# The order of the first transfers: gates by three queues, first words on two, then values and GpSimd's clearing of memory

## The chip, the cores and the metric

The kernel runs on one core of a Trainium2 chip. The metric is the device time of the whole kernel in microseconds (us), as the median of several executions. One more execution is taken with the hardware profiler; the span of its instructions and the durations of single operations come from that one.

## The reference

Four sequences, eight heads, 768 positions, head size 48. A recurrence with a complex gate for each position and head dimension makes the attention output, and a feed-forward block with a squared ReLU follows. All inputs and the output are float32.

```python
mag = np.sqrt(a_re * a_re + a_im * a_im)
scale = np.minimum(mag, 0.999) / (mag + 1e-06)
a_re_n, a_im_n = a_re * scale, a_im * scale
for t in range(S):                                  # S = 768
    new_re = ar * S_re - ai * S_im                  # ar, ai: the gates at t
    new_im = ar * S_im + ai * S_re
    kv = np.einsum('bhd,bhe->bhde', k[:, :, t], v[:, :, t])
    S_re, S_im = (new_re + kv, new_im)
    y[:, :, t] = np.einsum('bhd,bhde->bhe', q[:, :, t], S_re)

x = y.transpose(0, 2, 1, 3).reshape(3072, 384)
h = np.maximum(x @ w_in, 0.0)                       # w_in 384 x 2048
out = h * h @ w_out                                 # w_out 2048 x 384
```

The two weight matrices reach the chip as 64-bit floats, that is as pairs of 32-bit words, and are turned into 32-bit floats on VectorE.

## The kernel before, in words

**Tiling.** A chunk is 128 positions of one sequence; a group is one chunk of each of two sequences. There are 24 chunks in 12 groups. The heads lie in pairs on the partitions: 64 rows for each of two heads, of which 48 hold head dimensions and the 16 left over (the `pads`) hold a third each of the fourth pair of heads. The tile `raw` holds the gates (real and imaginary), the queries and the keys of a group; `vt` holds the values, two tiles for each of two groups.

**A list of tokens.** The order of the work on every engine is written out by hand as one list of tokens, `FRONT`. `follow` calls one small function for each token, and each engine's queue gets its instructions in the order in which these functions issue them. The tokens that matter here, with a group's or block's number behind the letter:

- `l0.0` loads the gates of the first group (`load_parts` with part 0); `l0.1` and `i0.1` load its queries and keys, the first head's half on SP, the other on GpSimd (POOL). `l1`, `i1` load the next group whole.
- `v0`, `v1` load values (`load_values`), two transfers each on SP.
- `f0` to `f15` fetch a block of weight words: for w_in the upper partitions' half on SP with `f`, and the lower half on POOL with `j`. There are three buffers for blocks.
- `W0`... let ScalarE watch the size of a block's words (L600, L602); `D0`... decode a block on VectorE in five operations (L587, L589, L591, L594 and a sum, L480).
- `M0` loads ScalarE's table and `M1` turns the mask.
- `o0.k` is step k of a group's operands. `o0.0` squares the gates on ScalarE (L700), `o0.3` sums them on VectorE (L713), `o0.4` (L718) and `o0.5` (L722) are the first inverse and its square on ScalarE, `o0.7` is the inverse on VectorE (L480, L731). `o0.8`, `o0.9`, `o0.10` are the limit, the lessened factor and the grown factor on ScalarE (two L685 and L745), `o0.11` makes the gates (L751 to L755), `o0.22` is L764 to L767, `o0.13` the scan (L771), `o0.14` the keys (L776, L685).
- `a0.k` and `b0.k` are the steps of a group's two chunks: 0 the scores (L872), 1 to 4 the keys turned and copied to `kt` (L879, L883, L884), 5 the masking (L480), 6 the sums of values (L898), 7 the tokens (L907), 8 the products to be added (`add`, L919), 9 the new state.
- `F`, `H` and the capital letters behind them are the feed-forward block.

VectorE's list begins with some small fills, then `o0.3`, `o0.7`, `D0`, `o0.11`, `D1`, `o0.13` and so on. ScalarE begins with its share of the gates' transfers, then `M0`, `o0.0`.

**The first transfers.** The gates of one chunk and one head are a large transfer of 144 KB (48 rows) and two of 24 KB (the pads). SP issues those of the first head of each pair and ScalarE those of the other: twelve in all, six on each. SP goes on with the four value transfers (192 KB each), its half of `f0` (192, 96 and 96 KB), then its half of the queries and keys. Transfers from SP and ScalarE share eight semaphores, and those from POOL have eight others, so that each issue waits until the transfer that used its semaphore eight issues before has landed.

**What POOL does first.** It clears the last 16 columns of the four `vt` tiles (L487), makes the identity and the mask, and clears `qk`, `last`, `prod`, the states, `kt` and `begun` (L558 to L571). Then come its halves of `f0` and of the queries and keys.

The profile's lines are those of the kernel before; in the changed kernel most stand one line earlier.

Of the kernel before, what the change touches and what calls it, by code (L numbers as in the profile page):

```python
# [44 lines left out]
def gap_rows(hh, d):  # L45
    return slice(hh * ROWS + d, (hh + 1) * ROWS)
# [379 lines left out]
def quotient_path(ctx, tc, feat, vtok, w_in, w_out, w1, w2, out, n_seq, count):  # L426

    nc = tc.nc
    N, _, D, _, NP, C = feat.shape
    DM, FF = w_in.shape  # L430
# [11 lines left out]
    W = C + 2  # L442
# [18 lines left out]
    def rows(hh):  # L461
        return head_rows(hh, D)
# [7 lines left out]
    def pads(hh):  # L470
        return gap_rows(hh, D)
# [11 lines left out]
    raw = const.tile([P, 4, GC, NG, C], F32, name="raw")  # L483

    vt = [const.tile([C, DM + PAD], F32, name=f"vt{i}") for i in range(2 * GC)]
    for t in vt:
        nc.gpsimd.memset(t[:, DM:], 0.0)  # L487


    TWO_QUEUES = 3  # L490
# [1 line left out]
    def load_parts(gi, part=None, second=False):  # L492


        parts = [slice(A_RE, Q), slice(Q, V), slice(A_RE, V)][2 if part is None else part]
        queues = [nc.sync, nc.scalar if part == 0 else other if gi < TWO_QUEUES else nc.sync]
        if part != 0 and gi < TWO_QUEUES:
            queues[not second] = None
        for b, n in enumerate(groups[gi]):
            for hh, queue in enumerate(queues):  # L500
                if queue is None:
                    continue
                queue.dma_start(
                    out=raw[rows(hh), parts, b].rearrange("d x g t -> d x (g t)"),
                    in_=feat[n, hh, :, parts, 0:NG].rearrange("d x g t -> d x (g t)"))

                gap = raw[pads(hh), parts, b]
                rest = feat[n, hh].rearrange("(r g) x p t -> r x g p t", g=NG)[:, parts, :, NG]
                for i in range(min(gap.shape[1:3])):
                    at = (slice(None), i) if gap.shape[1] < NG else (slice(None), slice(None), i)  # L510
                    queue.dma_start(out=gap[at], in_=rest[at])
# [23 lines left out]
    def turn_mask(step):  # L535
        if step == 0:

            nc.scalar.activation(out=sums[:, 0:1], in_=tiny, func=AF.Abs_reciprocal_sqrt)
            return
        nc.scalar.copy(out=mask.rearrange("p (j n) -> p n j", j=L),  # L540
                       in_=plain.rearrange("p (n j) -> p n j", j=L))
        turned = pm.tile([C, C], F32, tag="m", name="turned")
        nc.tensor.transpose(turned, mask, ident)
        nc.scalar.copy(out=mask.rearrange("p (j n) -> p n j", j=L),
                       in_=turned.rearrange("p (n j) -> p n j", j=L))
# [8 lines left out]
    qk_of = [const.tile([P, 4, GC, NG, W], F32, name=f"qk{i}") for i in range(2)]  # L554
    last = [const.tile([P, 4, GC, W], F32, name=f"last{i}") for i in range(2)]
    prod = [const.tile([P, 3, GC, NP], F32, name=f"prod{i}") for i in range(2)]
    for t in qk_of:
        nc.gpsimd.memset(t[:, :, :, :, C:W], 0.0)  # L558

    states = [[const.tile([P, 2, NP, ROWS], F32, name=f"state{b}{i}") for i in range(2)]  # L560
              for b in range(GC)]
    for t in last + prod + states[0] + states[1]:
        nc.gpsimd.memset(t, 0.0)
    kt = [const.tile([C, NP, P], F32, name=f"kt{i}") for i in range(2)]
    for t in kt:
        nc.gpsimd.memset(t, 0.0)

    sums = const.tile([P, NGR], F32, name="sums")
    ends = const.tile([P, NGR, SEG], F32, name="ends")
    begun = const.tile([P, E], F32, name="begun")  # L570
    nc.gpsimd.memset(begun, 0.0)  # L571
    sizes = const.tile([P, 2, 2 * NBLK], F32, name="sizes")
    nc.vector.memset(sizes, 1.0)
    tiny = const.tile([P, 1], F32, name="tiny")
# [467 lines left out]
    def outputs(i, r):  # L1042
# [27 lines left out]


    FRONT = (
        "l0.0 M0 j0 v0 v1 f0 o0.0 l0.1 i0.1 o0.3 o0.1 o0.4 o0.5 o0.7 o0.2 M1 o0.8 D0 f1 j1 o0.9 "
        "o0.10 o0.6 o0.11 f2 j2 W0 W1 D1 o0.22 f3 j3 o0.12 W2 o0.13 o0.15 o0.14 f4 j4 W3 l1 i1 "
        "o0.16 W4 o0.17 D2 o0.18 o1.6 o0.19 f5 j5 o0.20 o1.0 W5 a0.1 o1.3 o0.21 o1.1 D3 a0.2 "
        "a0.3 o1.4 a0.4 a0.8 o1.5 o1.2 o1.7 f6 j6 b0.0 a0.9 o1.8 b0.1 b0.5 o1.9 b0.6 D4 b0.2 "
        "b0.3 b0.7 a0.0 b0.4 o1.10 W6 b0.8 o1.11 f7 j7 a0.5 o1.12 o1.22 a0.6 b0.9 o1.13 W7 v2 "
        "a0.7 o1.15 o1.14 g0 l2 i2 o1.16 F0.0 o1.17 F0.1 H0.0 D5 o1.18 F0.2 H0.1 o2.6 o1.19 f8 "
        "F0.3 H0.2 F0.4 H0.3 o1.20 o2.0 F0.5 H0.4 W8 a1.1 o2.3 o1.21 D6 a1.2 a1.3 o2.1 a1.4 "
        "a1.8 o2.4 o2.2 F0.6 D7 f9 H0.5 o2.5 a1.0 H0.6 a1.9 F0.7 a1.5 W9 f10 o2.7 a1.6 b1.1 "  # L1080
        "a1.7 D8 b1.0 o2.10 o2.8 H0.7 b1.5 o2.9 f11 b1.6 D9 b1.2 b1.3 b1.7 T0.0 b1.4 g1 W10 "
        "o2.11 T0.1 W11 f12 F1.0 D10 o2.12 o2.22 F1.1 H1.0 D11 T0.2 H1.1 f13 W12 F1.2 o2.15 "
# [61 lines left out]
    def ranges(step):  # L1144
# [35 lines left out]
        "f": fetch,  # L1180
        "j": lambda i: fetch(i, True),
        "i": lambda gi, part=None: load_parts(gi, part, True),
        "D": weights,
        "W": lambda i: watch(words_of[i], i) if i in words_of else None,
        "t": sum_weights,
        "l": load_parts,
        "v": load_values,
        "M": turn_mask,
        "K": ranges,
    }  # L1190
# [13 lines left out]
@with_exitstack  # L1204
def kernel(
    ctx: ExitStack,
    tc: tile.TileContext,
    feat: bass.AP,
    vtok: bass.AP,
    w_in: bass.AP,  # L1210
    w_out: bass.AP,
    out: bass.AP,
    n_seq: int,
):
    nc = tc.nc
    DM, FF = w_in.shape
    wts = ctx.enter_context(tc.tile_pool(name="wts", bufs=1))
    w1 = wts.tile([P, DM // P, FF], F32, name="w1")
    w2 = wts.tile([P, FF // P, DM], F32, name="w2")
    count = wts.tile([1, 1], I32, name="count")  # L1220
    quotient_path(tc, feat, vtok, w_in, w_out, w1, w2, out, n_seq, count)
    n_good = nc.values_load(count, min_val=0, max_val=P)
    with tc.If(n_good < P):
        decode_weights(tc, w_in, w_out, w1, w2, feat.shape[2])
        general_path(tc, feat, vtok, w1, w2, out, n_seq)
# [30 lines left out]
```

## Time and profile before

| | |
|---|---|
| median of 4 runs | 707.35 us (707.0 to 708.59) |
| profiled execution, its own time | 706.3 us |
| its span, first to last instruction | 704.6 us |
| mean granted TensorE clock | 0.986 |
| TensorE busy | 618.9 us (88%) |
| VectorE busy | 524.4 us (74%) |
| ScalarE busy | 386.3 us (55%) |
| GpSimd busy | 36.1 us (5%) |
| moved by DMA | 47.75 MB, mean 68 GB/s |

Times inside the program are counted from the start of the span. Shares are means over stages that differ: the first 100 us, in which the weights are decoded and the first group's operands are made, look unlike the rest. A timeline line has the start, the duration (of the whole run of equal instructions, "x4"), the engine, the source line, the operation with what it writes and reads, and in brackets the engine's idle time before it and what ended that. SPq, POOLq or ACTq mark the issue of a transfer on a queue; the transfer itself lands later. The trace also holds a record for each landing.

### The profile page before, as it was taken

Reading aid. Unit: us, or ns where it says so; the run is one execution under the profiler, and the core shown is the slowest. Engines: PE = TensorE matmul, PEld = TensorE weight load, DVE = VectorE, ACT = ScalarE, POOL = GpSimd, SP = SyncE. Lnnn points to the kernel's source line nnn. Section 1 sums busy time; section 2 is a strip of 40 time slices with the busy share of each in tenths; the row PEclk is TensorE's granted clock in tenths of the full one; section 3 lists DMA queues with packets and bytes.
Section 4 is the critical chain, followed back from the end, with each engine's and each line's share of the span. In section 5 each row is a group of like instructions: output and inputs, shape, how many; then the busy total and the mean of one; then the engine's idle time right before and its main releaser. Section 6 shows DMA issues by size and latency. Waiting matters only on the chain.

```text
span 704.6 us, 12510 instructions
## 1 busy us (share of the span) xinstructions
PE 618.9 (88%) x4955; PEld 544.1 (77%) x4955; DVE 524.4 (74%) x916; ACT 386.3 (55%) x684; POOL 36.1 (5%) x91
## 2 busy tenths in 40 slices
PE   0006489999889999999999999999999999999995
PEld 0005377776578898998999989989989989989895
DVE  1999999999699786896785885995986976872130
ACT  6638387744648537537457557366476475340330
POOL 6331200000000000000000000000000000000000
PEclk9999699999999999999999999999999999999999
DMA  6973634471334062061161051141240330110101
GB/s 168 189 135 77 142 74 142 148 111 39 68 76 64 5 97 68 2 134 30 29 113 23 29 113 25 53 93 20 75 80 11 86 71 9 29 23 2 29 1 28
DMA packets 44164, 47.75 MB, mean 68 GB/s; under 512 B 6016, under 2 KB 39104, under 8 KB 44096
## 3 DMA queue, kind: packets, MB, share of 16 engines
q1 hardware_dynamic: 41408, 41.35, 27.8%
q0 software_dynamic: 2208, 5.11, 3.7%
q8 instruction: 41, 0.67, 0.4%
q10 hardware_dynamic: 480, 0.39, 0.2%
q14 instruction: 27, 0.22, 0.1%
HBM read 36.18 MB, written 4.72 MB: 58 GB/s over the span
## 4 chain that ended last, share of the span: by engine, by line
PE 74%; DVE 14%; DMA 4%; ACT 4%; SPq 2%; issue 1%; DVEq 0%; ACTq 0%
PE h_ps L961 30%; PE o_ps L1038 26%; PE a_ps L872 6%; PE y L898 3%; PE y L864 3%; PE add L919 3%; DMA raw<-in_feat_dram 2%; DVE ab L480 2%; DVE pr L480 2%; PE tp L879 2%; DVE room L480 1%; PE o_ps L977 1%; DVE qk L480 1%; DMA words<-in_moe_w_in_dram 1%; DVE decoded L589 1%
## 5 line engine op out<-in xcount | busy, mean ns | idle before, releaser
L961 PE MATMUL h_ps<-x,w 128*128 128x256 f32 x1152 | 257.1, 383 | 6.8 <-DMA x<-x 6.8
L961 PEld LDWEIGHTS h_ps<-x,w 128*128 128x128 f32 x1152 | 220.0, 192 | 37.9 <-issue 6.0
L966 ACT ACTIVATE h<-h_ps 128x512 f32<-128x512 f32 x96 | 57.5, 599 | 103.5 <-PE h_ps L961 95.4
L1038 PE MATMUL o_ps<-w,h 128*128 128x192 f32 x640 | 111.1, 328 | 0.0
L1038 PEld LDWEIGHTS o_ps<-w,h 128*128 128x128 f32 x640 | 103.6, 190 | 1.8 <-issue 0.9
L480 DVE TENSOR_TENSOR pr<-ab 128x384 f32<-128x384 f32 (+2 forms) x168 | 66.4, 413 | 4.4 <-ACT ab L759 0.5
L967 ACT ACTIVATE h<-h 128x512 f32<-128x512 f32 x96 | 60.6, 631 | 3.0
L879 PE MATMUL tp<-ident,qk 128*128 128x128 f32 x120 | 22.0, 294 | 43.9 <-DVE qk L480 42.0
L480 DVE TENSOR_TENSOR a<-a_ps,mask 128x1024 f32<-128x1024 f32 x24 | 29.4, 1224 | 38.6 <-PE a_ps L872 38.4
L480 DVE TENSOR_TENSOR mix<-h 128x256 f32<-128x256 f32 x40 | 16.9, 423 | 53.6 <-ACT h L967 53.6
L1038 PE MATMUL o_ps<-w_sum,mix 128*128 128x192 f32 x320 | 55.8, 328 | 0.0
L1038 PEld LDWEIGHTS o_ps<-w_sum,mix 128*128 128x128 f32 x320 | 52.0, 190 | 1.1 <-DVE state L480 0.7
L879 PEld LDWEIGHTS tp<-ident,qk 128*128 128x128 f32 x120 | 13.6, 144 | 49.9 <-issue 42.9
L480 DVE TENSOR_TENSOR ab<-pr 128x192 f32<-128x192 f32 (+1 forms) x180 | 45.8, 277 | 4.6
L480 DVE TENSOR_TENSOR qk<-ab,qk 128x768 f32<-128x768 f32 x48 | 44.9, 957 | 0.9
L685 ACT ACTIVATE qk<-raw 128x768 f32<-128x768 f32 x24 | 36.7, 1530 | 15.1 <-DVE raw L480 8.9
L977 PE MATMUL o_ps<-w,h 128*128 128x384 f32 x128 | 42.4, 488 | 0.0
L872 PE MATMUL a_ps<-qk 48*128 48x128 f32 x576 | 39.6, 285 | 0.0
L685 ACT ACTIVATE ab<-raw 128x768 f32<-128x768 f32 x24 | 37.1, 1565 | 2.4 <-DVE qk L480 2.4
L872 PEld LDWEIGHTS a_ps<-qk 48*128 48x128 f32 x576 | 35.0, 192 | 4.2 <-issue 4.2
L480 DVE TENSOR_TENSOR room<-ab,carry 128x1344 f32<-128x1344 f32 x24 | 36.3, 1552 | 2.2 <-ACT carry L800 2.2
L977 PEld LDWEIGHTS o_ps<-w,h 128*128 128x128 f32 x128 | 24.1, 190 | 16.2 <-DVE w L480 0.7
(106 smaller groups left out, 805.7 us busy)
## 6 DMA issues: line engine op xcount, KB each, us to landing
raw<-in_feat_dram SPq DMA_DIRECT2D x40, 288.0 KB
words<-in_moe_w_out_dram SPq DMA_DIRECT2D x8, 768.0 KB
last<-qk SPq DMA_DIRECT2D x72, 64.5 KB
vt<-in_vtok_dram SPq DMA_DIRECT2D x24, 192.0 KB
out_dram<-o SPq DMA_DIRECT2D x24, 192.0 KB
raw<-in_feat_dram SPq DMA_DIRECT2D x120, 32.0 KB
words<-in_moe_w_in_dram POOLq DMA_DIRECT2D x8, 192.0 KB, 4.9
words<-in_moe_w_in_dram SPq DMA_DIRECT2D x8, 192.0 KB
```

The lines of the kernel that those rows point to most:

```text
L480: nc.vector.tensor_tensor(out=out, in0=in0, in1=in1, op=op)
L685: nc.scalar.activation(out=out.rearrange("p c j n -> p c n j"), func=AF.Copy, in_=in_.rearrange("p c (n j) -> p c n j", j=L), **kwargs)
L864: nc.tensor.matmul(ys[p_ % 2][crossed(hh, p_), p_ // 2], lhsT=states[b][1 - c_seq % 2][rows(hh), c, p_], rhs=operand(c, p_, rows(hh)), sta ...
L872: nc.tensor.matmul(ps[:, hh, p_], lhsT=operand(2 + c, p_, rows(hh)), rhs=operand(c, p_, rows(hh)), start=(c == RE), stop=(c == IM))
L879: nc.tensor.transpose(tp[:, g], operands[gi][:, 2 + c, b, g, 0:C], ident)
L898: nc.tensor.matmul(tiles["y"][p_ % 2][crossed(hh, p_), p_ // 2], lhsT=v[:, at:at + ROWS], rhs=tiles["am"][:, hh, p_], start=(first and p_ ...
L919: nc.tensor.matmul(add[rr, c, p_], lhsT=kt[c][:, p_, rr], rhs=v[:, at:at + D], start=True, stop=True)
L961: nc.tensor.matmul(ps[:, j], lhsT=w1[:, g, (2 * f + j) * P:(2 * f + j + 1) * P], rhs=x_of[i][:, g], start=(g == 0), stop=(g == NG - 1))
L966: nc.scalar.activation(out=h, in_=h_ps[i, f], func=AF.Relu)
L967: nc.scalar.activation(out=h, in_=h, func=AF.Square)
L977: nc.tensor.matmul(o_of[i, b], lhsT=tokens_of(i, f, b)[:, j], rhs=w2[:, k], start=(k == 0), stop=(k == NFB - 1))
L1038: nc.tensor.matmul(to, lhsT=x(k)[:, j], rhs=factor(z)[:, 2 * k + j], start=(z in (0, 1, 3) and k == j == 0), stop=(k == KH // 2 - 1 and j ...
```

## The change

Three things are changed, all in what is issued at the start.

1. The small transfers (pads) of the gates of the group's second chunk are issued by POOL and no longer by SP and ScalarE. SP and ScalarE then issue four transfers of the gates each and POOL four.
2. In the list, `f0 j0` follow the gates at once; then come the queries and keys, `f1 j1`, the clearing, `f2 j2`, and only then the values `v0`. `v1` stands behind `f3`.
3. The clearing of memory by POOL, `vt`'s columns included, becomes a step `M2` of the list, in another order (`begun` first), between POOL's halves of `f1` and `f2`. The identity and the mask stay ahead of all.

Apart from this two steps change place further back: `o1.5` comes ahead of `a0.4`, and `b0.2` ahead of `b0.5`. The order of VectorE's instructions stays as it was.

```diff
-    for t in vt:
-        nc.gpsimd.memset(t[:, DM:], 0.0)
...
                     in_=feat[n, hh, :, parts, 0:NG].rearrange("d x g t -> d x (g t)"))
 
+                if part == 0 and b:
+                    queue = nc.gpsimd
                 gap = raw[pads(hh), parts, b]
...
             nc.scalar.activation(out=sums[:, 0:1], in_=tiny, func=AF.Abs_reciprocal_sqrt)
+            return
+        if step == 2:
+
+            for t in ([begun] + [t[:, :, :, :, C:W] for t in qk_of] + last + [t[:, DM:] for t in vt]
+                      + kt + prod + states[0] + states[1]):
+                nc.gpsimd.memset(t, 0.0)
             return
...
-    for t in qk_of:
-        nc.gpsimd.memset(t[:, :, :, :, C:W], 0.0)
...
-    for t in last + prod + states[0] + states[1]:
-        nc.gpsimd.memset(t, 0.0)
...
-    for t in kt:
-        nc.gpsimd.memset(t, 0.0)
...
-    nc.gpsimd.memset(begun, 0.0)
...
-        "l0.0 M0 j0 v0 v1 f0 o0.0 l0.1 i0.1 o0.3 o0.1 o0.4 o0.5 o0.7 o0.2 M1 o0.8 D0 f1 j1 o0.9 "
-        "o0.10 o0.6 o0.11 f2 j2 W0 W1 D1 o0.22 f3 j3 o0.12 W2 o0.13 o0.15 o0.14 f4 j4 W3 l1 i1 "
-        "o0.16 W4 o0.17 D2 o0.18 o1.6 o0.19 f5 j5 o0.20 o1.0 W5 a0.1 o1.3 o0.21 o1.1 D3 a0.2 "
-        "a0.3 o1.4 a0.4 a0.8 o1.5 o1.2 o1.7 f6 j6 b0.0 a0.9 o1.8 b0.1 b0.5 o1.9 b0.6 D4 b0.2 "
...
+        "l0.0 M0 f0 j0 l0.1 i0.1 f1 j1 M2 f2 j2 v0 o0.0 o0.3 o0.1 o0.4 o0.5 o0.7 o0.2 M1 o0.8 "
+        "D0 o0.9 o0.10 o0.6 o0.11 W0 W1 D1 o0.22 f3 v1 j3 o0.12 W2 o0.13 o0.15 o0.14 f4 j4 W3 "
+        "l1 i1 o0.16 W4 o0.17 D2 o0.18 o1.6 o0.19 f5 j5 o0.20 o1.0 W5 a0.1 o1.3 o0.21 o1.1 D3 "
+        "a0.2 a0.3 o1.4 o1.5 a0.4 a0.8 o1.2 o1.7 f6 j6 b0.0 a0.9 o1.8 b0.1 b0.2 b0.5 o1.9 b0.6 "
...
```

## The prediction

> **What bounds the kernel now.** I read the page's tenths first, then the waits of VectorE (DVE), then the timeline of the first 30 us, and last the chain of waits up to 204 us.
>
> The page's tenths, one digit per 17.6 us:
>
> ```profile
> PE   0006489999889999999999999999999999999995
> DVE  1999999999699786896785885995986976872130
> DMA  6973634471334062061161051141240330110101
> ```
>
> TensorE is full only from the seventh slice on. In the first six VectorE shows 9s from the second slice: it sets the pace there, and everything that TensorE does later hangs on it. The first slice, 0 to 17.6 us, has a 1 for VectorE and a 6 for DMA. What VectorE waits for up to 70 us:
>
> ```profile
> DVE room L713 <- ACT room L700: 7.8, 1, 7.8
> DVE decoded L587 <- DMA words<-in_moe_w_in_dram: 4.5, 1, 4.5
> DVE room L480 <- ACT room L722: 2.1, 1, 2.1
> ```
>
> Three waits, all before 19 us: for the gates and ScalarE's squares, for the inverse, and 4.5 us for the first block of words. The timeline says where they come from:
>
> ```profile
> 1.97 1.89 POOL L563 MEMSET last<- 128x1040 f32 x2
> ...
> 3.89 1.95 POOL L563 MEMSET state<- 128x512 f32 x4
> ...
> 5.18 2.70 SPq L520 DMA_DIRECT2D vt<-in_vtok_dram  x4
> ...
> 7.37 1.80 POOL L633 DMA_DIRECT2D words<-in_moe_w_in_dram  x3
> ...
> 7.82 1.48 ACT L700 ACTIVATE room<-raw 128x1536 f32<-128x1536 f32 x1 [0.84 <-DMA vt<-in_vtok_dram]
> 7.93 1.58 SPq L633 DMA_DIRECT2D words<-in_moe_w_in_dram  x3
> ...
> 13.37 0.96 DVE L731 SCALAR_TENSOR_TENSOR z<-room,z 128x768 f32<-128x768 f32 x1
> ...
> 18.82 0.56 DVE L587 TENSOR_SCALAR decoded<-words 128x768 int32<-128x768 int32 x1 [4.49 <-DMA words<-in_moe_w_in_dram]
> ```
>
> The words are issued only at 7.4 (POOL, behind its memsets) and 7.9 us (SP, behind the four vt transfers), and the landing records put their last piece at 18.7 us. The gates land at 7.67, when ACT L700 can begin. From 18.82 to 62 us VectorE has no wait over 0.1 us, and the chain goes through it: each microsecond won ahead of 18.82 is handed on. From 104 us the chain is mostly TensorE's, with pieces of VectorE, ScalarE and DMA up to 204 us, each released by its predecessor and none by a clock.
>
> **The Trainium skill.** "DMA: Bandwidth & Descriptors", section on queues, rings and completion order, says that each DMA engine takes turns between the queues that have work. The trace agrees: from 8 to 15 us POOL's queue moved 24 to 107 KB in each us beside SP's 112 to 178. The same page's section on the GpSimd path puts the fixed cost of a transfer at some 2.0 us. Here the first POOL transfer (7.37) has its first packet at 8.91 and a first landing at 10.22, 2.9 us. "SBUF — State Buffer", section "Who interferes with whom", says that a VectorE operation in a two-port mode (tensor_scalar can be) and GpSimd lock each other out for a whole instruction. No stretch of the trace before has a memset beside such an operation, so I bound that below.
>
> **The change part by part.**
>
> *Gates by three queues.* Each chunk's gates are a large and two small transfers per head. SP and ACT used to issue all twelve; four waited for the landing of earlier ones (eight transfers can be out on their two queues), the last being issued at 4.84 and landing at 7.67. Now the four small ones of the second chunk go by POOL, and ACT and SP issue four each without a wait. The last large one, issued at 2.89, landed at 6.35. POOL reaches its four after the identity and the mask, about 1.8 us (vt's memsets, 0.25, are gone from in front): 4 x 0.52 (row L511 POOL) or 0.24 more with the first issue's price of 0.76, so to 3.9-4.1. With 2.9 us from an issue to its first landing, the last, issued near 3.4, lands about 6.7 to 7.2. ACT is ready before: its two small issues (1.21 us) are gone, so the table load (1.28) ends near 4.6. I take 6.9 us for the gates against 7.82: **-0.9**. Bounds: -1.5 (the large one alone decides, 6.35), +0.9 (POOL's land at 8.7, since some of its other transfers took 4.5 to 8 us in traffic).
>
> *First words on two queues, before the values.* SP's words now stand right after its four gates and wait only for the landing of the first three transfers (3.8 to 4.9), so about 4 to 5.6 us instead of 7.93; POOL's at 4 to 5.7 instead of 7.37. The block is 768 KB; the windows show 222 GB/s from 8 to 16 us: 3.5 us of data, with the second half of the features interleaved, so by 10.5 (11.5 at the worst). VectorE comes to the decode when the inverse is done: before, 6.51 us after L700 began (7.82 to 14.33), so now at 13.4. The words are there: **-4.5**, the whole wait. What is late next is the gates themselves. The sum so far is 5.4: the decode starts at 13.4 for 18.8.
>
> *Is the cover still there behind it?* Decode one (4.1 us) ends at 17.6; ScalarE's limit, lessened and grown factor, which came at 17.56 and 18.20, come at 16.6 and 17.3. Decode two starts at about 21.1 and needs block f1, which landed at 25.47. In front of it on POOL's queue lie 96 KB of gates, 384 of f0 and 384 of features; with f1's own 384 these last three took from 8.9 (first packet) to 23.1 before, 14.2 us. From 5.4 on they give 19.6, 1.5 us in time; SP's half is earlier, since 768 KB of values are out of its way. No cost taken; if POOL's queue starves, up to 2 us.
>
> *The clearing of memory.* Seventeen memsets, some 5.9 us (0.80 to 1.05 and 1.83 to 7.45), move on POOL from ahead of f0 to behind f1's issues, thus about 12.5 to 18.4. Behind them is f2's POOL half, issued at 18.68 before, now 18.4 to 20. It lands near 23; ScalarE watches it (W2) at 25, decode three wants it at 38. Who reads what is cleared comes later: begun at about 24 (cleared first), qk and prod at 38, kt and last at 50 or more. Nothing waits. But the first decode now lies beside them: its two tensor_scalar of 0.56 us can each wait for the rest of a memset (at most 0.95, row L563). I take **+0.4**, bounds 0 and +2.
>
> *The values later.* v0 goes behind f2 on SP, v1 behind f3's wait; they land by about 24 and 30, and TensorE first reads them at 59.5. Nothing. The next group's features are issued behind `keys` (34.76, now 29.6), landed at 46.7 and have 3.3 us of slack (ACT L685 ends at 48.5, L700 waits for VectorE until 51.85); 1.5 MB at the 153 GB/s of that window end near 40 to 43, needed at 45. No cost taken, bound 1.
>
> *Two pieces of order further back.* `o1.5` (L722, 0.86 and 0.20) now comes ahead of the second kt copy:
>
> ```profile
> 58.78 0.48 ACT L883 COPY kt<-tp 128x384 f32<-128x384 f32 x1 [0.30 <-PE tp L879]
> 59.16 0.30 ACT L884 COPY kt<-tp 128x96 f32<-128x96 f32 x1
> 59.28 0.86 ACT L722 ACTIVATE room<-z 128x768 f32<-128x768 f32 x1
> ```
>
> TensorE's `add` (59.55) begins some 0.7 us later, then the scores, which VectorE's masking waits for (64.48, with 0.14 idle before it). VectorE's own use of L722 gains nothing, as decode D3 holds it until 60.6. **+0.6**, bounds 0 and +0.8. `b0.2` ahead of `b0.5` puts a kt copy between ScalarE's two L685, whose results VectorE wants at 69.7: nothing.
>
> **Sum.** -0.9 - 4.5 + 0.4 + 0.6 = -4.4 us. Against the profiled execution, 706.3 (span 704.6 and 1.7 around it), that is 701.9. The median of the runs, 707.35, lies 1.05 higher, so 703.0.
>
> **Rivals.**
>
> *Gates late.* POOL's four small transfers land at 8.7. The decode starts at 15.2, the gain is 2.6: 704.8. For it: POOL's landings of 4.5 to 8.7 us on the words; against: the queue is empty then.
>
> *The stream is the bound.* f1's POOL half or the next features come 2 us late, as DMA is near full from 8 to 46 us. Gain 2.4: 705.0. For it the DMA row of 1.02 from 18 to 30; against it the 0.46 and 0.34 in the first 8 us, capacity that the change uses.
>
> *Absorbed.* A later wait for a transfer (148.5 us, 4.4 of DMA on the chain) doesn't move: within 1.4 of 707.35. Against: its issue hangs on `keys` of its group, which moves.
>
> *Slower.* The clearing is locked out by VectorE's two-port operations and holds f2's POOL half. W2 stands ahead of `keys` on ScalarE, and the next features behind `keys`. W2 began at 29.45; with 3.3 us of slack it hurts from 32.8 on. Three issues and a landing take some 6 us, so the clearing would have to end at 26.7, 14 us for 5.9. If it took 17, the time is 3 us longer than before: 710.4. VectorE's few tensor_scalar of 0.56 us speak against it.
>
> **How the numbers follow.** The sum 0.56, gates late 0.16, stream 0.12, absorbed 0.07, slower 0.09. Faster by over 0.2% (1.4 us, what a measurement of this kernel can tell): 0.84; within it 0.07; slower 0.09. The likeliest is 703.0. The bounds of the sum alone give 701.0 (memsets free, order free, gates 6.35) to 704.9. To leave out no more than two in ten the range reaches over the two rivals: 700.9 to 705.9.
>
> **What would show it.** First decode at about 13.4 us with no wait for words ahead of it; ACT L700 at 6.4 to 7.2; POOL's four small transfers from 1.8 us; the memsets at about 12.5 to 18.4; decode two without a wait near 21; the first scores' masking near 60. I am wrong if L700 begins after 8, if VectorE waits for words or next features between 20 and 50, or if the shift at 60 us isn't found at 204 us.

## The result, and the profile after

The changed kernel takes 706.6 us (median of 34 runs, 704.91 to 709.19) where the kernel before took 707.79 (55 runs on the same chips). The ratio is 0.9986, 95% interval 0.998 to 0.9992: about 1 us less, and within the 0.2% named in the prediction. The forecast was 703.0, with a range of 700.9 to 705.9. The profiled execution of the changed kernel took 706.51 us for 706.3 before, its span 704.8 for 704.6; the one of the kernel before was among its quicker ones, 1.05 us under its median of 707.35, so the difference of the medians can't be read from these two profiles.

The tenths of the page, in slices of 17.6 us:

```profile
PE   0006489999889999999999999999999999999995
DVE  4999999999699786896785885995985976872130
DMA  8873644460334053061061051151240340110101
```

VectorE has a 4 for a 1 in the first slice. Whatever it did earlier ought to be missing further on; yet TensorE's digits are the same, slice by slice. What VectorE waited for up to 70 us:

```profile
DVE room L712 <- ACT room L699: 7.5, 1, 7.5
DVE room L480 <- ACT room L721: 2.1, 1, 2.1
DVE a L480 <- PE a_ps L871: 0.8, 1, 0.8
```

The wait of 4.5 us for the words is gone, as predicted, and nothing of its size has come in its place. A list of waits alone would call this a gain of 4.5 us. The busy time says otherwise. The windows by stage: first the changed kernel,

```profile
0.00:20.00 20.00, 0.48 (x1) 0.18 (x1) 9.42 (x10) 13.43 (x16) 16.44 (x43) 1.00 0.90 179
20.00:55.00 35.00, 0.00 (x0) 0.00 (x0) 33.68 (x55) 17.99 (x35) 9.54 (x19) 1.00 0.77 146
```

then the kernel before:

```profile
0.00:20.00 20.00, 0.47 (x1) 0.18 (x1) 4.56 (x10) 11.28 (x13) 14.62 (x39) 1.00 0.71 173
20.00:55.00 35.00, 0.00 (x0) 0.00 (x0) 33.68 (x55) 20.05 (x37) 9.53 (x19) 1.00 0.80 149
```

After the length of the window come PE, PEld, DVE, ACT and POOL. Up to 20 us VectorE began the same ten instructions in both, but they took 9.42 us for 4.56. From 20 to 55 us it did the same 55 in the same 33.68 us. So one instruction or more became 4.9 us longer. The tile `decoded` up to 30 us in the changed kernel (shortest, median and longest of two, in ns):

```profile
L586 DVE TENSOR_SCALAR decoded<-words x2: 553/3022/5491, 13.9 to 26.4; 128x768 int32<-128x768 int32 x2
L590 DVE TENSOR_SCALAR decoded<-decoded x2: 559/560/560, 20.4 to 28.0; 128x768 int32<-128x768 int32 x2
```

The same operation on the same shape took 5491 ns the first time and 553 the second. The timeline shows what lay beside the first:

```profile
3.87 1.60 POOL L632 DMA_DIRECT2D words<-in_moe_w_in_dram  x3
...
7.46 1.48 ACT L699 ACTIVATE room<-raw 128x1536 f32<-128x1536 f32 x1 [2.72 <-DMA raw<-in_feat_dram]
...
13.15 0.76 POOL L544 MEMSET begun<- 128x768 f32 x1
...
13.89 5.49 DVE L586 TENSOR_SCALAR decoded<-words 128x768 int32<-128x768 int32 x1
13.98 1.89 POOL L544 MEMSET last<- 128x1040 f32 x2
...
17.02 1.95 POOL L544 MEMSET state<- 128x512 f32 x4
...
19.41 0.96 DVE L588 SCALAR_TENSOR_TENSOR decoded<-words,decoded 128x768 int32<-128x768 int32 x1
```

The decode starts at 13.89 instead of 18.82, 4.93 us earlier. Its first operation spans POOL's clearing and ends at 19.38, 0.41 us behind the last memset (17.02 + 1.95 = 18.97). Its second operation starts at 19.41; before, it started at 19.42. So the 4.93 us are spent. That they are spent to the last hundredth is chance: the end of the hold hangs on when GpSimd's clearing begins, and in another execution, further below, it came 0.93 us earlier.

### The profile page after: what moved, and what is told of

Same layout as the page of the kernel before. It is cut to its first block, busy times and chain, and to the rows that moved or that the text cites. A ratio compares the mean times of both kernels' runs of the same rounds, so it can differ in the third digit from the quotient of the medians.

```text
span 704.8 us, 12515 instructions
## 1 busy us (share of the span) xinstructions
PE 618.6 (88%) x4955; PEld 544.1 (77%) x4955; DVE 529.2 (75%) x916; ACT 386.4 (55%) x684; POOL 37.8 (5%) x95
## 4 chain that ended last, share of the span: by engine, by line
PE 75%; DVE 11%; DMA 6%; ACT 3%; SPq 1%; issue 1%; POOL 1%; DVEq 0%; ACTq 0%; POOLq 0%
PE h_ps L960 30%; PE o_ps L1037 26%; PE a_ps L871 7%; DMA words<-in_moe_w_in_dram 3%; PE y L897 3%; PE y L863 3%; PE add L918 3%; PE tp L878 2%; DVE ab L480 2%; DMA raw<-in_feat_dram 1%; DVE room L480 1%; DVE pr L480 1%; PE o_ps L976 1%; SPq L830 1%; DVE qk L480 1%
## 5 line engine op out<-in xcount | busy, mean ns | idle before, releaser
L480 DVE TENSOR_TENSOR pr<-ab 128x384 f32<-128x384 f32 (+2 forms) x168 | 66.4, 413 | 4.4 <-ACT ab L758 0.5
L480 DVE TENSOR_TENSOR a<-a_ps,mask 128x1024 f32<-128x1024 f32 x24 | 29.4, 1223 | 38.8 <-PE a_ps L871 38.8
L480 DVE TENSOR_TENSOR mix<-h 128x256 f32<-128x256 f32 x40 | 16.9, 423 | 53.6 <-ACT h L966 53.6
L480 DVE TENSOR_TENSOR ab<-pr 128x192 f32<-128x192 f32 (+1 forms) x180 | 45.8, 277 | 4.6
L480 DVE TENSOR_TENSOR qk<-ab,qk 128x768 f32<-128x768 f32 x48 | 44.9, 957 | 0.9
L480 DVE TENSOR_TENSOR room<-ab,carry 128x1344 f32<-128x1344 f32 x24 | 36.3, 1552 | 2.2 <-ACT carry L799 2.2
```

What stands on the lines that cost most here:

```text
L480: nc.vector.tensor_tensor(out=out, in0=in0, in1=in1, op=op)
```

## The experiments

Theory A: GpSimd's memsets hold VectorE's `tensor_scalar` until their whole unbroken run is over. The other theories are in the expectations. A **shift** below is the start of a VectorE instruction less its start in the kernel before; the masking is the first one (L480 on `a_ps`, 64.48 before). Edits are against the changed kernel unless said.

### The clearing on VectorE

```diff
-                nc.gpsimd.memset(t, 0.0)
+                nc.vector.memset(t, 0.0)
```

> The changed kernel, with its seventeen memsets on VectorE (ahead of its first sum of squares, where it is idle until 8.98 us) and none on GpSimd. Theory (lock): GpSimd's run of memsets, 13.15 to 18.97 us, kept VectorE's first tensor_scalar of the first decode from running (5.49 us for 0.56). Without them it takes 0.56, the second operation starts near 14.5 for 19.41, and the 4.9 us are handed on to the end: profile shift at the scan -4.9, whole time about 4.9 below the changed kernel's 706.6, so 701.7, ratio to the kernel before 0.991 to 0.992. Rival (words): the tensor_scalar was slow because its words or the memory were still busy with incoming transfers; then it still takes over 3 us and the time stays within 1 us of the changed kernel. Rival (stream): the first decode is early, but the second waits for f1 or the scan is held by later transfers, and less than half of the 4.9 us is left at 50 us.

Measured: 703.11 us for 707.73 before, ratio 0.994 (0.9922 to 0.9959), span 701.4. The timeline:

```profile
13.81 0.55 DVE L586 TENSOR_SCALAR decoded<-words 128x768 int32<-128x768 int32 x1
14.40 0.96 DVE L588 SCALAR_TENSOR_TENSOR decoded<-words,decoded 128x768 int32<-128x768 int32 x1
```

The first operation is back to 0.55 us, at the same place, and the shift is -5.01 at the first decode and up to 55 us. VectorE's memsets lie from 1.59 to 7.99 us, where it waits for the gates anyway. I had expected 701.7 for this version; a part of the 5 us is lost behind 55 us (see "Why the prediction was wrong"). That 703.11 meets the 703.0 of the prediction is therefore luck. And POOL's queue lost its memsets too, so this run alone doesn't tell a hold from a queue that is freer.

### The same clearing, and operations of another form

The memsets stay on GpSimd. Only the first block's two `tensor_scalar` get a second input in memory, with the same result (`bits` is a constant tile):

```diff
+        if j == 0:
+            nc.vector.scalar_tensor_tensor(out=head, in0=high, scalar=3,
+                                           in1=bits[:, 0:1].to_broadcast([P, E]),
+                                           op0=ALU.logical_shift_left, op1=ALU.bitwise_and)
...
+            nc.vector.scalar_tensor_tensor(out=rest, in0=head, scalar=-2 ** 23, in1=head,
+                                           op0=ALU.bitwise_and, op1=ALU.bitwise_and)
```

> The changed kernel, with the two tensor_scalar operations of the first decode alone written as scalar_tensor_tensor with two inputs in SBUF (0.96 us each for 0.56); the memsets stay on GpSimd beside it. Theory (lock by the two-port form): these two run at 0.96 us beside the memsets, the first decode takes some 5 us from 13.9, gain 4.9 - 0.8 = 4.1 us at the scan, time about 702.5, ratio 0.993. Rival (any VectorE operation that comes while GpSimd clears memory is held): the first operation again ends at about 19 us and the time is that of the changed kernel plus 0.4 to 0.8.

Measured: 703.96 for 707.73, ratio 0.9951 (0.9933 to 0.9968), span 702.3. The timeline:

```profile
13.51 0.95 DVE L589 SCALAR_TENSOR_TENSOR decoded<-words,bits 128x768 int32<-128x768 int32 x1
13.54 1.89 POOL L544 MEMSET last<- 128x1040 f32 x2
...
15.49 0.96 DVE L598 SCALAR_TENSOR_TENSOR decoded<-decoded 128x768 int32<-128x768 int32 x1
15.54 1.01 POOL L544 MEMSET kt<- 128x512 f32 x2
```

Beside the same memsets (12.72 to 18.52 us here) the two operations take 0.95 and 0.96 us and nothing holds them. POOL's work and its queue are as in the changed kernel, so it is the form of VectorE's operation that decides, not the queue and not the memory being busy. The time is again above what I had expected (702.5).

### The same hold in the kernel before

To the kernel before, with its order of transfers and its own clearing, the same 17 memsets are added a second time, behind POOL's half of `f1`:

```diff
+        if step == 2:
+            for t in ([begun] + [t[:, :, :, :, C:W] for t in qk_of] + last + [t[:, DM:] for t in vt]
+                      + kt + prod + states[0] + states[1]):
+                nc.gpsimd.memset(t, 0.0)
+            return
...
-        "l0.0 M0 j0 v0 v1 f0 o0.0 l0.1 i0.1 o0.3 o0.1 o0.4 o0.5 o0.7 o0.2 M1 o0.8 D0 f1 j1 o0.9 "
+        "l0.0 M0 j0 v0 v1 f0 o0.0 l0.1 i0.1 o0.3 o0.1 o0.4 o0.5 o0.7 o0.2 M1 o0.8 D0 f1 j1 M2 o0.9 "
```

> The kernel before, with the same seventeen memsets issued on GpSimd a second time, right behind its half of f1, where the first decode begins (18.8 us). Theory (lock): the first tensor_scalar (18.82) is held until the run of memsets ends, near 24.4, 5.6 us for 0.56, and VectorE is some 5 us later from there to the end: 712 to 713, ratio 1.007. Behind the run f2's half is 5.9 us later, which the watch of that block (29.45) and the third decode (43) cover. Rival (the stall belongs to the changed order of transfers): the decode runs at its 4.1 us, and the time is within 0.7 us of before.

Measured: 712.05 for 707.73, ratio 1.0069 (1.005 to 1.0088), span 709.9. The timeline:

```profile
18.33 0.76 POOL L543 MEMSET begun<- 128x768 f32 x1
...
18.33 6.22 DVE L592 TENSOR_SCALAR decoded<-words 128x768 int32<-128x768 int32 x1 [4.82 <-DMA words<-in_moe_w_in_dram]
...
22.19 1.94 POOL L543 MEMSET state<- 128x512 f32 x4
...
24.59 0.96 DVE L594 SCALAR_TENSOR_TENSOR decoded<-words,decoded 128x768 int32<-128x768 int32 x1
```

As expected (712 to 713): without any of the change's transfers the hold is there, 6.22 us for 0.56, again ending 0.42 us behind the last memset (24.13). The shift of +5.17 stays to the end (span +5.3). This shows also that a microsecond lost ahead of 20 us is lost in the whole time.

### The clearing in two pieces

`begun`, `qk` and `last` are cleared ahead of POOL's half of `f2`, the rest behind it (step `M3`):

```diff
-        "l0.0 M0 f0 j0 l0.1 i0.1 f1 j1 M2 f2 j2 v0 o0.0 o0.3 o0.1 o0.4 o0.5 o0.7 o0.2 M1 o0.8 "
+        "l0.0 M0 f0 j0 l0.1 i0.1 f1 j1 M2 f2 j2 M3 v0 o0.0 o0.3 o0.1 o0.4 o0.5 o0.7 o0.2 M1 o0.8 "
```

> The changed kernel with GpSimd's memsets in two pieces: five (begun, qk, last; some 2.9 us) ahead of its three issues for f2, and twelve (vt, kt, prod, the states; some 3.2 us) behind them. Theory A (VectorE's two-port operation is held as long as one memset follows another on GpSimd): the first tensor_scalar of the first decode, which starts near 13.9 us beside the first piece, ends when that piece does, near 16.5, and not at the end of all memsets; its second tensor_scalar (near 17.5) may be held by the second piece, up to 20.7. Theory B (held for one memset only): it ends by 15 us. Theory C (held until GpSimd has nothing more): it ends near 20.7. Time under A between 704 and 707.

Measured: 704.35 for 708.04, ratio 0.9937 (0.9914 to 0.996), span 702.9. The timeline:

```profile
12.89 1.89 POOL L544 MEMSET last<- 128x1040 f32 x2
13.47 1.79 DVE L586 TENSOR_SCALAR decoded<-words 128x768 int32<-128x768 int32 x1
14.71 1.69 POOL L632 DMA_DIRECT2D words<-in_moe_w_in_dram  x3
...
16.29 0.56 DVE L590 TENSOR_SCALAR decoded<-decoded 128x768 int32<-128x768 int32 x1
...
16.38 0.57 POOL L544 MEMSET vt<- 128x16 f32 x4
```

The first piece ends at 14.78 and the operation at 15.26: the hold is 1.2 us, and it ends although POOL goes on, now with issues of DMAs. So it is the end of the memsets that lets VectorE in (theory A): it came while the first of the two `last` memsets ran and was held by the second too, against theory B, and it did not wait for POOL's second piece, against theory C. The second `tensor_scalar` came 0.09 us ahead of the second piece and took its plain 0.56; this time it was the small `vt` memsets that took 0.57 for the 0.27 of an undisturbed four. In these traces the engine that came first held the other.

### The clearing in front

Two places ahead of the first decode, both still on GpSimd: right behind the gates, and behind POOL's half of `f0`.

```diff
-        "l0.0 M0 f0 j0 l0.1 i0.1 f1 j1 M2 f2 j2 v0 o0.0 o0.3 o0.1 o0.4 o0.5 o0.7 o0.2 M1 o0.8 "
+        "l0.0 M0 M2 f0 j0 l0.1 i0.1 f1 j1 f2 j2 v0 o0.0 o0.3 o0.1 o0.4 o0.5 o0.7 o0.2 M1 o0.8 "
```

```diff
-        "l0.0 M0 f0 j0 l0.1 i0.1 f1 j1 M2 f2 j2 v0 o0.0 o0.3 o0.1 o0.4 o0.5 o0.7 o0.2 M1 o0.8 "
+        "l0.0 M0 f0 j0 M2 l0.1 i0.1 f1 j1 f2 j2 v0 o0.0 o0.3 o0.1 o0.4 o0.5 o0.7 o0.2 M1 o0.8 "
```

> The changed kernel with the clearing alone put back: GpSimd's memsets stand behind its four transfers of the gates and ahead of its half of f0, all else as changed. Theory: they run from 3.9 to about 9.7 us, when VectorE does nothing in a two-port form, so that the first tensor_scalar takes 0.56. GpSimd's half of f0 is issued from 9.7 and lands near 14 to 15.5 (2.9 to 4.5 us after the first issue): the first decode starts 0 to 1.7 us later than the 13.9 us of the changed kernel, and ends near 19 for 22.96. The second decode may then wait for GpSimd's half of f1 (issued some 5 us later than in the changed kernel, landing near 22 to 24; wanted at 22). Time 703 to 705. Rival (the clearing in front of f0 costs as much as its lock): the words land at 17.5 or later and the time is that of the changed kernel, 706.6.

> The changed kernel with the clearing one place earlier than in the change: behind GpSimd's half of f0, ahead of its halves of queries, keys and f1. Theory: memsets from 5.5 to 11.3 us, over before the first tensor_scalar (13.9), which takes 0.56; the first decode runs from 13.9 to 18.0. GpSimd's halves of queries and keys are issued from 11.3 and those of f1 from about 15, landing near 21 to 24: the second decode (wanted at 21.4) waits up to 2.5 us. Gain at the scan 2.5 to 5 us, time 702.5 to 705. Rival (what is pushed back on GpSimd's queue is as dear as the lock): f1 lands after 25.5 and the time is 706 or more.

Both missed the theory, and the times are nearer to the rivals' (though in front of `f0` the words came at 15.75 and not at 17.5 or later). In front of `f0`: 707.48 for 707.34, ratio 0.9999 (0.9985 to 1.0012). Behind it: 706.74 for 707.34, ratio 0.9989 (0.998 to 0.9999). The first operation of decodes one and two, with the clearing in front of `f0`:

```profile
15.75 0.56 DVE L586 TENSOR_SCALAR decoded<-words 128x768 int32<-128x768 int32 x1 [1.47 <-DMA words<-in_moe_w_in_dram]
...
25.93 0.56 DVE L586 TENSOR_SCALAR decoded<-words 128x768 int32<-128x768 int32 x1 [2.52 <-DMA words<-in_moe_w_in_dram]
```

and behind it:

```profile
13.91 0.55 DVE L586 TENSOR_SCALAR decoded<-words 128x768 int32<-128x768 int32 x1
...
25.39 0.56 DVE L586 TENSOR_SCALAR decoded<-words 128x768 int32<-128x768 int32 x1 [3.82 <-issue]
```

There is no hold in either (0.56, 0.55), but the wait for words has come back. POOL clears for 5.8 us and what it issues behind that comes so much later: with the clearing behind `f0`, the last piece of `f1` landed at 25.21 instead of 19.57, and decode two stood still for 3.82 us. The profile calls this "issue"; by its landing it is the transfer. The clearing in one piece on GpSimd thus costs its time at each of the three places: as late words in front, as a hold behind. In two pieces, or beside operations of the other form, it did not (704.35 and 703.96).

### The two pieces of order back

```diff
-        "a0.2 a0.3 o1.4 o1.5 a0.4 a0.8 o1.2 o1.7 f6 j6 b0.0 a0.9 o1.8 b0.1 b0.2 b0.5 o1.9 b0.6 "
-        "D4 b0.3 b0.7 a0.0 b0.4 o1.10 W6 b0.8 o1.11 f7 j7 a0.5 o1.12 o1.22 a0.6 b0.9 o1.13 W7 "
+        "a0.2 a0.3 o1.4 a0.4 a0.8 o1.5 o1.2 o1.7 f6 j6 b0.0 a0.9 o1.8 b0.1 b0.5 o1.9 b0.6 "
+        "D4 b0.2 b0.3 b0.7 a0.0 b0.4 o1.10 W6 b0.8 o1.11 f7 j7 a0.5 o1.12 o1.22 a0.6 b0.9 o1.13 W7 "
```

> The changed kernel with o1.5 and b0.2 back in their old places of the list; all else as changed. Theory: the shift of +0.68 us that VectorE shows from its first masking (64.48 to 65.17) on is gone, the shift at 200 us is about 0.0 against the kernel before, the time 0.5 to 0.7 us below the changed kernel: ratio near 0.998. Rival: the +0.68 comes from elsewhere (values that land later), and it stays.

Measured: 706.61 for 707.73, ratio 0.9988 (0.9975 to 1.0), no different from the changed kernel. The lines for TensorE's `add` and VectorE's first decode:

```profile
13.60 4.85 DVE L586 TENSOR_SCALAR decoded<-words 128x768 int32<-128x768 int32 x1
...
58.60 1.95 PE L918 MATMUL add<-vt,kt 128*64 128x48 f32 x32 [0.81 <-ACT kt L883]
```

`add` stands at 58.60 for 59.55 before, a shift of -0.95, the same as VectorE's in this execution (-0.94). In the changed kernel it stood at 60.09 with VectorE unshifted. The delay of 0.54 us that `o1.5` puts on it is thus shown. What it is worth in the whole time isn't: the scores behind it ran slower here (2.93 us for 2.69 in the changed kernel), and the masking shifts by only -0.17.

This run shows one more thing. POOL's clearing began at 12.23, not 13.15, because the landing that POOL's last issue of `f1` waits for came earlier, and so the hold ended earlier (4.85 us). Up to 55 us the two kernels issue the same, so the end of the hold differs from one execution to the next by about 1 us. Whether that bears on the difference of 1 us between the medians isn't shown, and these two traces speak against a simple link: the execution whose hold ended earlier has the longer span (705.6 for 704.8).

### Clearing on VectorE and the order back

The edit of the last experiment and the first one's together:

```diff
-                nc.gpsimd.memset(t, 0.0)
+                nc.vector.memset(t, 0.0)
...
-        "a0.2 a0.3 o1.4 o1.5 a0.4 a0.8 o1.2 o1.7 f6 j6 b0.0 a0.9 o1.8 b0.1 b0.2 b0.5 o1.9 b0.6 "
...
+        "a0.2 a0.3 o1.4 a0.4 a0.8 o1.5 o1.2 o1.7 f6 j6 b0.0 a0.9 o1.8 b0.1 b0.5 o1.9 b0.6 "
...
```

> The changed kernel with the memsets on VectorE and, besides, o1.5 and b0.2 back in their old places. With the memsets alone on VectorE, VectorE was 5.0 us earlier up to 60 us, and TensorE's first add 4.5 (55.04 for 59.55): ScalarE's L721 stood ahead of its kt copy. Theory: the add is now 5.0 us earlier, and the first masking gains the same 0.5; time 0.5 below the 703.1 of the clearing on VectorE, 702.6, ratio 0.9930 to 0.9936. Rival (TensorE's clock decides the first scores, 2.93 us for the first 24 matmuls against 2.55): the add starts earlier, but the total moves by less than 0.3.

Measured: 702.56 for 708.04, ratio 0.9908 (0.9888 to 0.9928), with 702.6 expected. It is the lowest time of all, ahead of both kernels. `add` comes at 54.41 for 55.04 with the clearing on VectorE alone, and the shift at the masking is -4.36 for -3.73. The intervals of the two versions just overlap, and the profiled execution, the slowest of five, has a span of 702.6 for 701.4. So the 0.6 us are seen at the masking and not settled in the whole time.

### The gates back on two queues

The version above without POOL's share of the gates:

```diff
-                if part == 0 and b:
-                    queue = nc.gpsimd
```

> As dve_order_back, with all twelve transfers of the gates on SP and ScalarE again (six each), none on GpSimd. Theory (POOL's four transfers take a real part off): ScalarE's first squares begin 0.4 to 0.9 us later than the 7.1 to 7.5 us of the kernels with three queues, and the whole is as much later: 703.0 to 703.5. Rival (no gain, as the gates are bound by what the queues move): the squares begin between 7.0 and 7.8 as well, and the time is within 0.3 of dve_order_back.

Measured: 707.46 for 708.04, ratio 0.9991 (0.998 to 1.0002). All of the gain is gone, which neither the theory (0.4 to 0.9 us) nor the rival had. ScalarE's first work on the gates:

```profile
11.92 1.48 ACT L697 ACTIVATE room<-raw 128x1536 f32<-128x1536 f32 x1 [4.84 <-DMA words<-in_moe_w_in_dram]
```

The gates land at 11.7 us. SP and ScalarE issue their last small ones at 6.2 and 5.0 us, because four must wait for earlier landings, and POOL's words, now issued from 1.67 us, are on their way by then. With the early words the third queue is worth 11.92 - 7.31 = 4.6 us (7.31 is L699 in the version above): it issues the gates sooner, and it keeps POOL's words behind them. The second part can be told from the first on the last large transfer, which SP issues at 2.89 or 2.90 us in both: by the landing records it was complete at 6.84 us with POOL's gates ahead, and at 8.93 with POOL's words ahead.

### TensorE kept busy ahead of the first scores

The version with the clearing on VectorE and the order back, and in it 15 matmuls (128 x 384) whose result nobody uses, from about 43 us:

```diff
+        if step == 4:
+            warm = pm.tile([P, NG, C], F32, tag="m", name="warm")
+            for _ in range(15):
+                nc.tensor.matmul(warm, lhsT=ident, rhs=qk_of[1][:, 3, 0, :, 0:C], start=True, stop=True)
+            return
...
-        "l1 i1 o0.16 W4 o0.17 D2 o0.18 o1.6 o0.19 f5 j5 o0.20 o1.0 W5 a0.1 o1.3 o0.21 o1.1 D3 "
+        "l1 i1 o0.16 W4 o0.17 D2 o0.18 o1.6 M4 o0.19 f5 j5 o0.20 o1.0 W5 a0.1 o1.3 o0.21 o1.1 D3 "
```

> As dve_order_back, with 15 matmuls (128x384, their result unused) on TensorE from about 43 us, where it is idle until 50.8 us. Theory: of the 5.0 us that VectorE is early at 55 us, a part is lost because TensorE's matmuls run at half pace up to 81 us (first 24 of the scores 2.93 us, and again 2.93 the second time where the kernel before needs 2.55 and 1.61). With TensorE busy beforehand the first scores take near 1.6 us and the first masking comes 1 to 2 us earlier: time 700.5 to 701.7. Rival (the pace isn't set by earlier work, or the full clock is lost again in the gaps): the scores still take 2.93, and the time is that of dve_order_back, or up to 2 us more if the matmuls run late and hold the first transposes.

Measured: 707.91 for 708.04, ratio 0.9986 (0.9966 to 1.0005): all that the version without them had gained (702.56) is gone. TensorE:

```profile
42.49 12.80 PE L543 MATMUL warm<-qk,ident 128*128 128x384 f32 x30 [28.96 <-ACT qk L689]
55.35 0.55 PE L883 MATMUL tp<-ident,qk 128*128 128x128 f32 x3
...
59.41 2.93 PE L876 MATMUL a_ps<-qk 48*128 48x128 f32 x24
```

The 12.80 us were longer than I had sized them and held up the turned keys (55.35 us; without the added matmuls 50.71). They did bring the full rate: the trace's records of the granted clock have it from 48.3 to 58.5 us, and the keys took 0.55 us. Without them the same line reads

```profile
50.71 0.87 PE L878 MATMUL tp<-ident,qk 128*128 128x128 f32 x3 [36.67 <-DVE qk L480]
```

But at 58.5 us the clock fell back to half, 0.9 us ahead of the scores, and these took the slow 2.93 us all the same. So the rival held in its second form, the full clock lost again. From 55.0 to 58.5 us TensorE was busy for 1.92 of 3.5 us; that these gaps are the cause isn't shown.

## Why the prediction was wrong

**The step that failed is the price of the clearing beside the first decode**, put at +0.4 with a bound of 2. The prediction took each `tensor_scalar` to wait for the rest of one memset, at most 0.95 us. Measured, the first waited for all that was left of the run of seventeen: 5.49 - 0.56 = 4.93 us. Three traces give the same rule: the operation ended 0.41, 0.42 and 0.42 us behind the last memset (changed kernel, added clearing, order back), which is most of its own 0.56. In two pieces the hold shrank to the first piece, and an operation with two inputs in memory wasn't held at all. With 4.93 for 0.4 the prediction's own sum gives -4.4 + 4.5 = +0.1. With all terms as measured, -4.93 for gates and words, +4.93 for the hold and +0.68 for the order, it gives +0.68, and VectorE's shift is about +0.7 from the first masking on to 500 us; the span shows +0.2.

The Trainium skill's "SBUF — State Buffer", section "Who interferes with whom", which I had used for the bound, says that whoever issues first gets the shared pair for the whole instruction. The lock is there, but the measurement goes further: back-to-back memsets kept it over the whole run. The same section says that a VectorE operation with two inputs contends with a GpSimd instruction that reads memory, not with one that only writes. A memset only writes, and 0.95 us beside the memsets agrees.

The bounds were added wrongly besides: the four terms at their bounds give 701.4 to 706.6, not 701.0 to 704.9. That the upper end is the measured time is chance, as the gates, the words and the order were not at their bounds and the hold was beyond its own. Of the signs to watch, the three of being wrong don't catch the hold, as they watch for waits and the hold is busy time. Decode two does: I expected it near 21 us, and it came at 26.40.

**The rival "absorbed" has the measured time** (within 1.4 us of 707.35) **without its cause.** It had the gain swallowed by a transfer at 148.5 us; it was gone at 19.4.

**The rival "slower" had the right mechanism on the wrong engine.** It took VectorE to lock out the clearing. In the changed kernel POOL came first by 0.74 us (13.15 against 13.89). Split, with VectorE ahead by 0.09, it was POOL that waited, for some 0.3 us.

The other steps:

- **Words, -4.5: right.** No wait for words ahead of the decode. The last piece of the first block landed at 11.60, later than the 10.5 (11.5 at the worst) of the prediction, but it was wanted only at 13.89.
- **Gates, -0.9: sized too high.** L699 began at 7.46 for 7.82, so -0.36 instead of -0.9. POOL's last small transfer landed at 7.24, at the upper end of my 6.7 to 7.2. The 2.9 us from issue to landing were read wrongly: 10.22 is the first of the sixteen landing records of that transfer, and the last came at 15.77, 8.4 us after the issue. POOL's four small ones were complete after 3.5 to 4.0 us. The last large one came later too, at 7.06 for 6.35. Across the versions with three queues L699 lies from 6.79 to 7.76; the old start gave 7.82 and 7.01. The gain against the old start is not clear of this scatter. Against two queues with early words it is 4.6 us, a side that I hadn't priced.
- **The cover behind: right.** POOL's half of `f1` landed at 18.96 (19.6 predicted). SP's half, which I had earlier than that, came at 19.57. Decode two had no wait, and the memsets stood at 13.15 to 18.97 (12.5 to 18.4 predicted). Readers of the cleared tiles and the third block were not late.
- **Order, +0.6: right at the masking.** `add` +0.54, masking 65.17 for 64.48, +0.68. Where the first scores ran slow (2.93 us), VectorE lost 1.3 us up to the masking in the five traces with the new order and 0.7 to 0.8 in the three with the old one (the version with the added matmuls apart), the same 0.6.
- **"Each microsecond won ahead of 18.82 is handed on": only in part.** A loss was handed on (+5.17 at the start, +5.3 at the end). Of a gain of 5.01 at 55 us, 3.73 was left at the first masking and 3.2 in the span. TensorE's scores, in the kernel before and then with the clearing on VectorE:

```profile
61.43 2.55 PE L872 MATMUL a_ps<-qk 48*128 48x128 f32 x24
...
67.27 1.61 PE L872 MATMUL a_ps<-qk 48*128 48x128 f32 x24
```

```profile
56.92 2.93 PE L871 MATMUL a_ps<-qk 48*128 48x128 f32 x24
...
64.77 2.93 PE L871 MATMUL a_ps<-qk 48*128 48x128 f32 x24
```

Started 4.5 us earlier, the same matmuls run at about half the rate twice. The records of the granted clock agree: the first stretch at full rate begins at 63.45 us before and at 81.65 here. More is lost near 105 us, where every trace has a stretch at half rate. In the four traces besides the kernel before where it lasts 3.4 us, VectorE's shift changes by at most 0.24 us between 105 and 115; in the seven where it lasts 6.8 us, VectorE falls back by another 0.7 to 1.6 us. All versions with the clearing on VectorE are among the seven. That the clock is the cause of this second loss is not shown; the two go together in all of them. So even with the hold taken away the forecast of -4.4 was some 1 us too good in the profile (span -3.2 for this version), though the time of the runs came to 703.1.

## What to carry to other kernels

When work moves to a quiet engine, ask what it will lie beside, and price a shared resource by the whole unbroken run of the other engine's instructions, not by one of them. A wait that has vanished from the list of waits may sit inside an instruction: compare the busy time of the same instructions in the same window, and look for one operation with a longest duration far from its shortest. GpSimd's idle share of 95% did not make its 5.8 us of clearing free: in one piece it cost words in front of the decode and a hold beside it. Three things took most of that away: an engine that was waiting, operations of another form beside it, and a cut in the run of memsets.

## What the hardware did that I had not expected

- A VectorE `tensor_scalar` of 0.56 us took 5.49, 6.22 and 4.85 us beside an unbroken run of GpSimd memsets, 1.79 beside a run that ended for DMA issues, and 0.55 when no memset lay beside it. The memsets of the first three took no longer for it (5.8 us for the seventeen).
- Word transfers issued early on POOL's queue delayed the gates on the other two queues. A large one that SP issued at 2.89 us was complete at 8.93 us there and between 6.08 and 7.14 in the eleven other traces; the last of the gates landed at 11.7 us there, and near 7.2 where POOL's share of the gates stood ahead of its words.
- TensorE's full rate came as late as 81.6 us (first record of the granted clock, with the clearing on VectorE) for 63.4 before, although TensorE was busy for 14.5 of the 15 us from 55 to 70. The Trainium skill's "TensorE: Matmul & The Clock Gate", Part 1, has the full clock after a busy window of about 3.4 us; this trace does not agree. The added matmuls did bring the full rate, recorded from 48.3 us, 5.8 us after they began; it was gone again at 58.5. What sets the moment stays open.
